# Output rows of odd batches tiled from row 64 on, and tail tiles stored by one DMA over 128 partitions

## The chip, the cores and the metric

The kernel runs on one core of a Trainium2 chip. The metric is device time in microseconds (us), the median of several executions of the same program. One further execution is recorded by the hardware profiler; the profile and the trace are of that one.

## The reference

Eight batches of 576 positions pass through eight heads of linear attention (head width 64), and the result (8 x 576 x 512) through a spectral mixer.

```python
# attention, phi(x) = elu(x) + 1
kv  = einsum('bhsd,bhse->bhde', phi(k), v);  z = sum(phi(k), axis=2)
x   = einsum('bhsd,bhde->bhse', phi(q), kv) / (einsum('bhsd,bhd->bhs', phi(q), z) + 1e-6)
# mixer, on x as [batch, 576, 512]
X   = rfft(x, axis=1)                 # the first 64 modes are kept
Y_m = X_m @ (w_r[m] + 1j * w_i[m])    # 64 modes, 512 x 512 each, complex
u   = x + irfft(Y)
out = u + relu(u @ w_ch)              # float32
```

The mode weights are the bulk of the input: 128 matrices of 512 x 512.

## The kernel before

**Row tiles.** A batch has 576 rows. Its first 512 are cut into four main tiles of 128: tile `jj` holds rows jj, jj+4, jj+8 and so on, so that one partition of `x_main[b]` holds four consecutive rows. The last 64 rows of two neighbouring batches share one tail tile: the even batch in partitions 0 to 63, the odd batch in partitions 64 to 127. `x_tail[i // 2]` holds two tail tiles side by side in a partition. There are 32 main and 4 tail tiles.

**First part (up to about 105 us).** Batch by batch, q, k and v are loaded by POOL's DMA queue, the features are formed, and q is turned (`qT`). `form_x` (L250) multiplies `qT` with the batch's kv, and its L262 takes the reciprocal of the denominators into `rd_all[b]`, row by row in the tiling above. `transform` makes the 64 Fourier modes of x from this.

**Modes (L335).** The weights stream in by POOL's queue (L115), 512 KB per half mode, into eight buffers, after twelve early ones. A load is issued when PE has used the buffer it goes to. For each mode PE multiplies the real and the imaginary weights (L348), DVE or ACT copies the result out (L362 or L364), and PE sorts it into `YT` (L366). The last four modes are in a fixed order, with filler matmuls (L333) between their halves. Mode 63 is done in another form (L386).

**Channel products (L466).** Between the modes, for each of the 36 tiles, PE multiplies `qT` with kv once more (L146), DVE divides by multiplying with `rd_all` (L479), ACT casts (L486), PE transposes (L489), DVE copies out (L491), PE multiplies with w_ch (L494) and ACT copies the product out (L502). The place of these instructions among those of the modes is chosen by a scheduler from its own costs and the waits; each engine then runs its own list strictly in order. Only what is marked as kept in program order stays where the source has it.

**Row products (L509).** Once modes 0 to 55 are in `YT`, each batch's rows are multiplied with w_ch (L517) and transposed (L521) into `YZ[b]`: 56 modes, real and imaginary, make 112 partitions. The last eight modes follow after mode 63 (L658, L668) and are distributed by eight small DMAs (L672).

**Output (L605).** For each of 18 pairs of tiles, PE adds E (L577) and the inverse transform of the second half of `YZ` (L536) in PSUM, ACT applies relu (L588), PE adds the inverse transform of the first half (L536), DVE adds x (L617 or L622), and `store` (L590) writes the pair. The inverse transform's matrix `inv_sb` is the stationary operand; its columns are sorted so that a tile takes 128 (or, for each half of a tail tile, 64) adjacent ones. The 16 pairs of main tiles leave by SP's queue, one DMA each, but the first and last pair in two; the two pairs of tail tiles leave in two DMAs each, of 64 partitions:

```python
for hf in range(2):
    (nc.sync, nc.gpsimd)[hf].dma_start(
        out=out[2 * i + hf : 2 * i + 4 : 2, 512:S, :].rearrange("b r d -> r b d"),
        in_=x_tail[i // 2][hf * 64 : hf * 64 + 64, :, :],
    )
```

The tail pairs come before the last main pair of batches 3 and 7.

Of the kernel before, what the change touches and what calls it, by code (L numbers as in the profile page):

```python
# [10 lines left out]
F32 = mybir.dt.float32  # L11
# [5 lines left out]
NJ = 9  # L17
NP = 64


def _dft_consts(S: int, NM: int, NL: int, NB: int):

    m = np.arange(NM)
    s_cols = np.concatenate([4 * np.arange(128) + jj for jj in range(4)] + [512 + np.arange(NP)])
    s_rows = np.concatenate([s_cols, s_cols[512:]]).reshape(5, 128).T
    ang = 2.0 * np.pi * s_rows[:, :, None] * m / S
    fwd = np.concatenate([np.cos(ang), -np.sin(ang)], axis=2)

    scale = np.where(m == 0, 1.0, 2.0) / S
    ang = 2.0 * np.pi * np.outer(m, s_cols) / S  # L30
    inv = np.empty((NM, 2, S), dtype=np.float64)
    inv[:, 0, :] = np.cos(ang) * scale[:, None]
    inv[:, 1, :] = -np.sin(ang) * scale[:, None]
    pick = np.zeros((128, 16), dtype=np.float16)
    for quad in range(4):
        for c in range(16):
            pick[quad * 32 + c, c] = 1.0

    inv0 = np.zeros((NL, 2, NB, S), dtype=np.float64)
    inv0[:, :, 0, :] = inv[NM - NL :]  # L40
    return (
        fwd.astype(np.float16), inv.reshape(2 * NM, S).astype(np.float16),
        inv0.reshape(2 * NL * NB, S).astype(np.float16), pick,
    )
# [3 lines left out]
def kernel(  # L48
# [10 lines left out]
    nc = tc.nc  # L59

    B, H, S, Dh = q.shape
# [4 lines left out]
    NJJ = 4  # L66
# [38 lines left out]
    kv_all = [xpool.tile([128, 2, 2, 65], F16, tag="kv", bufs=B, name=f"kv{b}") for b in range(B)]  # L105
    rd_all = [xpool.tile([128, 5, 2, 4], F32, tag="rd", bufs=B, name=f"rd{b}") for b in range(B)]
# [29 lines left out]
        pool, tag, bufs = (wpool, "w", W_KEEP) if kk < n_keep else (wpre, "wp", W_PRE)  # L136
        w_in.setdefault(kk, []).append(w_load(kk, half, pool, tag, bufs))

    def num_matmuls(num, orow, qT, kv_sb, jj, pinned=False):
        cols = slice(jj, 512, NJJ) if jj < NJJ else slice(512, NJ * NP)  # L140
        for hpp in range(2):
            for h2 in range(2):
                for hpo in range(2):
                    rows = slice(hpo * 64, hpo * 64 + 64)
                    c0 = (hpp * 2 + h2) * 65
                    mm = nc.tensor.matmul(  # L146
                        num[hpo][orow, c0 : c0 + 65], qT[rows, hpp, h2, cols], kv_sb[rows, hpp, h2, :]
                    )
                    if pinned:
                        pin(mm)  # L150
        return [n[orow, 0:260].rearrange("p (c n) -> p c n", c=4) for n in num]

    def q_view(t):
        return t.rearrange("p (c t s) -> p c t s", c=2, t=2)

    qT_all = [q_tile(f"qT{b}") for b in range(B)]
# [93 lines left out]
    def form_x(b, jj):  # L250
        if jj == 0:
            x16s[b] = (
                sA.tile([128, NJJ, D], F16, tag="x16", bufs=2, name=f"x16_{b}"),
                sA.tile([128, D], F16, tag="x16t", bufs=2, name=f"x16t_{b}"),
            )
        tail = jj == NJJ
        orow = HALVES[b % 2] if tail else slice(0, 128)
        num = psA.tile([128, 2, 512], F32, tag="big", bufs=3, name=f"num{b}_{jj}")
        num_matmuls([num[:, o] for o in range(2)], orow, q_view(qT_all[b]), kv_all[b], jj, True)
        nv = num[orow, :, 0:260].rearrange("p o (c n) -> p o c n", c=4)  # L260
        rden = rd_all[b][orow, jj]
        pin(nc.vector.reciprocal(out=rden, in_=nv[:, :, :, 64]))  # L262
        dst = x16s[b][1][orow, :] if tail else x16s[b][0][:, jj, :]
        pin(
            nc.vector.tensor_tensor(  # L265
                out=dst.rearrange("p (o c d) -> p o c d", o=2, c=4),
                in0=nv[:, :, :, 0:64],
                in1=rden.unsqueeze(3).broadcast_to([64 if tail else 128, 2, 4, Dh]),
                op=ALU.mult,
            )  # L270
        )
# [162 lines left out]
    for kk in range(n_early):  # L434
# [3 lines left out]
    sW = ctx.enter_context(tc.tile_pool(name="sW", bufs=1))  # L438
    x_main = [sW.tile([128, NJJ, D], F32, tag="x_main", bufs=B, name=f"x_main{b}") for b in range(B)]
    x_tail = [  # L440
        sW.tile([128, 2, D], F32, tag="x_tail", bufs=B // 4, name=f"x_tail{i}") for i in range(B // 4)
    ]
    YZ = [sW.tile([128, 2, D], F16, tag="YZ", bufs=B, name=f"YZ{b}") for b in range(B)]
    E0: dict[int, object] = {}

    def x_of(t: int):
        if t < B * NJJ:
            return x_main[t // NJJ][:, t % NJJ, :]
        i = t - B * NJJ
        return x_tail[i // 2][:, i % 2, :]  # L450
# [10 lines left out]
    def bank(name: str, shape=(128, D), dtype=F32):  # L461
        return psB.tile(list(shape), dtype, tag="bank", bufs=4, name=name)
# [3 lines left out]
    def channel_product(t: int):  # L466

        num = [bank(f"nw{t}_{o}") for o in range(2)]
        tail = t >= B * NJJ
        if tail:  # L470
            i = t - B * NJJ
            parts = [(2 * i + h, NJJ, slice(h * 64, h * 64 + 64)) for h in range(2)]
        else:
            parts = [(t // NJJ, t % NJJ, slice(0, 128))]
        x = x_of(t)
        for b, jj, orow in parts:
            nv = num_matmuls(num, orow, q_view(qT_all[b]), kv_all[b], jj)
            for o in range(2):
                nc.vector.tensor_tensor(  # L479
                    out=x[orow, o * 256 : o * 256 + 256].rearrange("p (c d) -> p c d", c=4),  # L480
                    in0=nv[o][:, :, 0:64],
                    in1=rd_all[b][orow, jj, o].unsqueeze(2).broadcast_to([64 if tail else 128, 4, Dh]),
                    op=ALU.mult,
                )
        x16 = sW.tile([128, D], F16, tag="x16w", bufs=2, name=f"x16w{t}")
        nc.scalar.copy(out=x16, in_=x)  # L486
        xT_ps = bank(f"xTp{t}", [128, NDC, 128], F16)
        for c in range(NDC):
            nc.tensor.transpose(xT_ps[:, c, :], x16[:, c * 128 : c * 128 + 128], id16)  # L489
        xT = sW.tile([128, NDC, 128], F16, tag="xTw", bufs=2, name=f"xTw{t}")  # L490
        nc.vector.tensor_copy(out=xT, in_=xT_ps)  # L491
        e_ps = bank(f"eps{t}")
        for c in range(NDC):
            nc.tensor.matmul(  # L494
                e_ps, xT[:, c, :], wch16[:, c, :], start=(c == 0), stop=(c == NDC - 1)
            )
        need = {t // NJJ} if not tail else {2 * i, 2 * i + 1}
        for b in sorted(need):
            if b not in E0:
                E0[b] = q_tile(f"E0_{b}")  # L500
        for cols, dst in e0_parts(t):
            nc.scalar.copy(out=dst, in_=e_ps[:, cols])  # L502
# [29 lines left out]
    def add_inverse(n: int, i: int, t: int, half: int, what: int = BOTH):  # L532

        acc = accs[n][:, i]
        mm = lambda o, l, r: on_bank(
            n, {i}, nc.tensor.matmul(o, l, r, start=False, stop=True, skip_group_check=True)  # L536
        )
        if t < B * NJJ:
            parts = [(t // NJJ, slice(0, 128), slice(t % NJJ * 128, t % NJJ * 128 + 128))]
        else:  # L540
            p = t - B * NJJ
            parts = [(2 * p + h, slice(h * 64, h * 64 + 64), slice(512, 576)) for h in range(2)]
        for b, r, sel in parts:
            if what == BOTH:
                mm(acc[r, :], inv_sb[:, sel], YZ[b][:, half, :])
                continue
            if what & EARLY:
                mm(acc[r, :], inv_sb[: 2 * NE, sel], YZ[b][: 2 * NE, half, :])
            if what & LATE:
                mm(acc[r, :], inv0_sb[:, sel], last[:, half, :])  # L550
# [39 lines left out]
    def store(t: int, n_t: int):  # L590
        if t < B * NJJ:
            b, jj = divmod(t, NJJ)
            nc.sync.dma_start(
                out=out[b, 0:512, :].rearrange("(r j) d -> r j d", j=NJJ)[:, jj : jj + n_t, :],
                in_=x_main[b][:, jj : jj + n_t, :],
            )
            return
        i = t - B * NJJ
        for hf in range(2):
            (nc.sync, nc.gpsimd)[hf].dma_start(  # L600
                out=out[2 * i + hf : 2 * i + 4 : 2, 512:S, :].rearrange("b r d -> r b d"),
                in_=x_tail[i // 2][hf * 64 : hf * 64 + 64, :, :],
            )

    def finish(n: int):  # L605
        acc = accs[n]
# [47 lines left out]
    for h in range(2):  # L654
        cols = slice(h * hw, h * hw + hw)
# [67 lines left out]
```

## Time and profile before

| | |
|---|---|
| median of 4 runs | 432.47 us (431.88 to 433.25) |
| the profiled execution | 433.15 us, of which the profile's span is 431.2 us |
| busy share of the span | PE 70%, PE weight loads 36%, DVE 41%, ACT 34%, POOL 22% |
| DMA moved | 92.38 MB, mean 214 GB/s |
| mean granted TensorE clock | 0.708 |
| stores of x_main | 14 of 512 KB and 4 of 256 KB on SP |
| stores of x_tail | 2 of 256 KB on SP, 2 of 256 KB on POOL |

PE is TensorE's matmul stream and PEld its weight loads; DVE is VectorE, ACT ScalarE, POOL GpSimd; SP only issues DMAs here. A line such as L494 is a line of the kernel above. In the forty slices of the span a digit is a share in tenths. The granted clock is the share of TensorE's full clock. A line of the timeline gives the start, the duration, the engine, the source line, what is written and read, and the count; the bracket at its end is the engine's idle time before it, with what ended it.

### The profile page before, as it was taken

Reading aid. Unit: us, or ns where it says so; the run is one execution under the profiler, and the core shown is the slowest. Engines: PE = TensorE matmul, PEld = TensorE weight load, DVE = VectorE, ACT = ScalarE, POOL = GpSimd, SP = SyncE. Lnnn points to the kernel's source line nnn. Section 1 sums busy time; section 2 is a strip of 40 time slices with the busy share of each in tenths; the row PEclk is TensorE's granted clock in tenths of the full one; section 3 lists DMA queues with packets and bytes.
Section 4 is the critical chain, followed back from the end, with each engine's and each line's share of the span. In section 5 each row is a group of like instructions: output and inputs, shape, how many; then the busy total and the mean of one; then the engine's idle time right before and its main releaser. Section 6 shows DMA issues by size and latency. Waiting matters only on the chain.

```text
span 431.2 us, 6233 instructions
## 1 busy us (share of the span) xinstructions
PE 301.4 (70%) x2551; PEld 154.1 (36%) x2551; DVE 176.6 (41%) x333; ACT 146.9 (34%) x227; POOL 92.8 (22%) x167
## 2 busy tenths in 40 slices
PE   0358676787028777676776778777787758998991
PEld 0346555673004233322322223223232217834340
DVE  1699998954004232322232223223223312201893
ACT  3687666621003222222223222222222311301781
POOL 4232322222112221211222112112112121210100
PEclk9999866665558766657568565555556666998997
DMA  8999999999999999999999999999999999993797
GB/s 147 207 208 209 209 209 209 212 213 216 221 211 213 215 213 213 214 213 213 213 215 214 213 212 215 213 214 214 213 213 213 215 214 213 214 212 73 295 328 278
DMA packets 35707, 92.38 MB, mean 214 GB/s; under 512 B 3168, under 2 KB 16480, under 8 KB 35680
## 3 DMA queue, kind: packets, MB, share of 16 engines
q0 software_dynamic: 32160, 82.52, 98.4%
q1 hardware_dynamic: 3520, 9.47, 6.0%
q8 instruction: 20, 0.33, 0.3%
q14 instruction: 7, 0.06, 0.0%
HBM read 164.07 MB, written 9.44 MB: 402 GB/s over the span
## 4 chain that ended last, share of the span: by engine, by line
DMA 68%; PE 16%; DVE 6%; issue 5%; ACT 2%; POOL 1%; DVEq 0%; POOLq 0%; ACTq 0%
DMA wi<-in_moe_w_i_dram 35%; DMA wr<-in_moe_w_r_dram 21%; PE P L348 4%; DMA pick_sb<-row_pick 4%; DMA q<-in_q_dram 4%; PE acc L536 3%; DMA k<-in_k_dram 3%; PE z L517 2%; DVE x L265 2%; PE acc L577 2%; PE eps L494 1%; PE yp L521 1%; PE yt L366 1%; DVE qe L195 1%; ACT ke L182 1%
## 5 line engine op out<-in xcount | busy, mean ns | idle before, releaser
L494 PE MATMUL eps<-wch,xTw 128*128 128x512 f16 x144 | 62.7, 585 | 3.4 <-DVE xTw L491 3.2
L502 ACT CAST E<-eps 128x512 f16<-128x512 f32 (+1 forms) x40 | 21.3, 544 | 121.0 <-PE eps L494 121.0
L348 PE MATMUL P<-wi,xt_c 128*32 128x512 bf16 x252 | 45.5, 565 | 22.2 <-DMA wi<-in_moe_w_i_dram 22.1
L115 POOL DMA_DIRECT2D wi<-in_moe_w_i_dram x65 | 34.5, 532 | 121.7 <-PE P L348 83.1
L348 PE MATMUL P<-wr,xt_c 128*32 128x512 bf16 x252 | 45.3, 577 | 21.8 <-DMA wr<-in_moe_w_r_dram 19.9
L115 POOL DMA_DIRECT2D wr<-in_moe_w_r_dram x64 | 34.0, 532 | 120.0 <-PE P L348 93.7
L479 DVE TENSOR_TENSOR x_main<-nw,rd 128x256 f32<-128x256 f32 x64 | 24.2, 420 | 73.1 <-PE nw L146 73.0
L362 DVE CAST ys<-P 128x512 f16<-128x512 f32 x32 | 22.0, 688 | 60.3 <-PE P L348 60.2
L348 PEld LDWEIGHTS <-xt_c 128*32 128x32 bf16 x504 | 24.0, 163 | 57.6 <-issue 28.8
L146 PEld LDWEIGHTS <-qT 64*128 64x128 f16 (+1 forms) x640 | 21.4, 126 | 55.7 <-issue 40.1
L364 ACT CAST ys<-P 128x512 f16<-128x512 f32 x31 | 18.2, 586 | 62.0 <-PE P L348 61.7
L366 PE MATMUL yt<-pick_sb,ys 128*128 128x16 f16 x252 | 16.8, 177 | 30.7 <-DMA pick_sb<-row_pick 20.4
L491 DVE COPY xTw<-xTp 128x512 f16<-128x512 f16 x36 | 15.2, 423 | 43.9 <-PE xTp L489 43.9
L366 PEld LDWEIGHTS <-ys 128*128 128x128 f16 x252 | 12.9, 105 | 51.1 <-issue 24.3
L146 PE MATMUL num<-kv,qT 64*128 64x65 f16 (+1 forms) x320 | 13.8, 227 | 23.2 <-ACT kv L242 20.1
L494 PEld LDWEIGHTS <-xTw 128*128 128x128 f16 x144 | 14.6, 123 | 38.1 <-issue 22.2
L182 ACT ACTIVATE qe<-q 128x1152 f16<-128x1152 f16 x16 | 17.7, 1156 | 22.4 <-DMA q<-in_q_dram 22.4
L211 PE MATMUL qTp<-id,qe 128*128 128x128 f16 x144 | 16.5, 309 | 12.1 <-DVE qe L195 11.7
L486 ACT CAST x16w<-x_main 128x512 f16<-128x512 f32 x32 | 19.8, 619 | 13.4 <-DVE x_main L479 13.4
L265 DVE TENSOR_TENSOR x<-num,rd 128x512 f16<-128x512 f32 x32 | 22.1, 692 | 1.1
L489 PE MATMUL xTp<-id,x16w 128*128 128x128 f16 x144 | 19.4, 278 | 4.0 <-ACT x16w L486 3.6
L588 ACT ACTIVATE acc<-acc 128x512 f32<-128x512 f32 x36 | 19.1, 581 | 5.5 <-PE acc L536 3.8
(69 smaller groups left out, 385.0 us busy)
## 6 DMA issues: line engine op xcount, KB each, us to landing
wr<-in_moe_w_r_dram POOLq DMA_DIRECT2D x64, 512.0 KB, 18.3
wi<-in_moe_w_i_dram POOLq DMA_DIRECT2D x63, 512.0 KB, 18.4
out_dram<-x_main SPq DMA_DIRECT2D x14, 512.0 KB, 5.0
q<-in_q_dram POOLq DMA_DIRECT2D x8, 576.0 KB, 13.1
k<-in_k_dram POOLq DMA_DIRECT2D x8, 576.0 KB, 14.5
v<-in_v_dram POOLq DMA_DIRECT2D x8, 576.0 KB, 16.7
out_dram<-x_main SPq DMA_DIRECT2D x4, 256.0 KB, 3.6
wch<-in_moe_w_ch_dram POOLq DMA_DIRECT2D x1, 512.0 KB, 20.4
```

What stands on the lines that cost most here:

```text
L115: tc.keep_in_program_order(nc.gpsimd.dma_start(out=w[:, dcs], in_=rows_of[:, dcs, :]))
L146: mm = nc.tensor.matmul(num[hpo][orow, c0 : c0 + 65], qT[rows, hpp, h2, cols], kv_sb[rows, hpp, h2, :])
L182: pin(nc.scalar.activation(out=ev[:, c], in_=heads(nm, b)[:, c], func=AF.Exp))
L265: nc.vector.tensor_tensor(out=dst.rearrange("p (o c d) -> p o c d", o=2, c=4), in0=nv[:, :, :, 0:64], in1=rden.unsqueeze(3).broadcast_to([ ...
L348: mm = nc.tensor.matmul(P[i][dc * 32 : dc * 32 + 32, :], xt_cols(dc, t, kk), w[:, dc, i * pw : i * pw + pw], start=(t == 1), stop=(t == 0) ...
L362: nc.vector.tensor_copy(out=dst, in_=P[i])
L366: mm = nc.tensor.matmul(yt_ps[:, ec, kk % 8, :], st[:, ec * 128 : ec * 128 + 128], pick_sb)
L479: nc.vector.tensor_tensor(out=x[orow, o * 256 : o * 256 + 256].rearrange("p (c d) -> p c d", c=4), in0=nv[o][:, :, 0:64], in1=rd_all[b][or ...
L486: nc.scalar.copy(out=x16, in_=x)
L489: nc.tensor.transpose(xT_ps[:, c, :], x16[:, c * 128 : c * 128 + 128], id16)
L494: nc.tensor.matmul(e_ps, xT[:, c, :], wch16[:, c, :], start=(c == 0), stop=(c == NDC - 1))
L502: nc.scalar.copy(out=dst, in_=e_ps[:, cols])
```

## The change

Odd batches' main tiles start at row 64 (`BASE`), and their remaining rows are 0 to 63. In the flat view of the output (`out_rows`, 4608 rows), the last 64 rows of an even batch and the first 64 of the next are adjacent, so a tail tile is 128 consecutive rows. Each tail pair is stored by one DMA on SP; POOL stores nothing.

The first part keeps its tiling for all batches, so the stored reciprocals no longer match the odd batches' tiles: their channel products take their own, one `[128, 4]` (or 64 rows) reciprocal per half, 40 in all. `inv_sb` is no longer sorted; a main tile takes every fourth column of it, from row 64 on for odd batches.

```diff
-    ang = 2.0 * np.pi * np.outer(m, s_cols) / S
+    ang = 2.0 * np.pi * np.outer(m, np.arange(S)) / S
...
-    def num_matmuls(num, orow, qT, kv_sb, jj, pinned=False):
-        cols = slice(jj, 512, NJJ) if jj < NJJ else slice(512, NJ * NP)
+    def rows_of(jj: int, base: int = 0):
+
+        if jj < NJJ:
+            return slice(base + jj, base + 512, NJJ)
+        return slice(512, S) if base == 0 else slice(0, base)
+
+    def num_matmuls(num, orow, qT, kv_sb, cols, pinned=False):
...
-        num_matmuls([num[:, o] for o in range(2)], orow, q_view(qT_all[b]), kv_all[b], jj, True)
+        num_matmuls(
+            [num[:, o] for o in range(2)], orow, q_view(qT_all[b]), kv_all[b], rows_of(jj), True
+        )
...
+    BASE = (0, 64)
+    out_rows = out.rearrange("b s d -> (b s) d")
...
-            nv = num_matmuls(num, orow, q_view(qT_all[b]), kv_all[b], jj)
+            nv = num_matmuls(num, orow, q_view(qT_all[b]), kv_all[b], rows_of(jj, BASE[b % 2]))
             for o in range(2):
+                rden = rd_all[b][orow, jj, o]
+                if b % 2 == 1:
+                    rden = sW.tile([128, 4], F32, tag="rdw", bufs=4, name=f"rdw{t}_{o}")[orow]
+                    nc.vector.reciprocal(out=rden, in_=nv[o][:, :, 64])
                 nc.vector.tensor_tensor(
...
-                    in1=rd_all[b][orow, jj, o].unsqueeze(2).broadcast_to([64 if tail else 128, 4, Dh]),
+                    in1=rden.unsqueeze(2).broadcast_to([64 if tail else 128, 4, Dh]),
...
-            parts = [(t // NJJ, slice(0, 128), slice(t % NJJ * 128, t % NJJ * 128 + 128))]
+            b, jj = divmod(t, NJJ)
+            parts = [(b, slice(0, 128), rows_of(jj, BASE[b % 2]))]
...
-            parts = [(2 * p + h, slice(h * 64, h * 64 + 64), slice(512, 576)) for h in range(2)]
+            parts = [
+                (2 * p + h, slice(h * 64, h * 64 + 64), rows_of(NJJ, BASE[h])) for h in range(2)
+            ]
...
+            r0 = b * S + BASE[b % 2]
             nc.sync.dma_start(
-                out=out[b, 0:512, :].rearrange("(r j) d -> r j d", j=NJJ)[:, jj : jj + n_t, :],
+                out=out_rows[r0 : r0 + 512, :].rearrange("(r j) d -> r j d", j=NJJ)[:, jj : jj + n_t, :],
...
-        for hf in range(2):
-            (nc.sync, nc.gpsimd)[hf].dma_start(
-                out=out[2 * i + hf : 2 * i + 4 : 2, 512:S, :].rearrange("b r d -> r b d"),
-                in_=x_tail[i // 2][hf * 64 : hf * 64 + 64, :, :],
-            )
+        nc.sync.dma_start(
+            out=out_rows.rearrange("(i r) d -> r i d", i=B // 2)[512:640, i : i + 2, :],
+            in_=x_tail[i // 2],
+        )
```

## The prediction

> **What bounds the kernel now.** I read first the page's forty slices, to see which resource is full when.
>
> ```profile
> PEclk9999866665558766657568565555556666998997
> DMA  8999999999999999999999999999999999993797
> GB/s 147 207 208 209 209 209 209 212 213 216 221 211 213 215 213 213 214 213 213 213 215 214 213 212 215 213 214 214 213 213 213 215 214 213 214 212 73 295 328 278
> ```
>
> The DMA engines are full for 36 of 40 slices: this is the weight stream, at one fixed rate of 213 GB/s (by the trace one 512 KB load lands every 2.45 us, without a gap, the last at 394.06). Slice 37 is the hand-over (73 GB/s), and the last three store the output. So the end is set by three things: the arrival of the last weights, what lies between them and the first store, and the stores. Next, the windows by stage (us, busy time and count of PE, PEld, DVE, ACT, POOL, then granted clock, DMA share, GB/s).
>
> ```profile
> 346.50:357.00 10.50, 5.72 (x36) 2.07 (x36) 1.81 (x3) 1.17 (x2) 2.11 (x4) 0.66 1.06 213
> 357.00:364.00 7.00, 6.80 (x25) 4.89 (x26) 1.11 (x3) 1.17 (x2) 0.53 (x1) 0.52 1.06 212
> 364.00:379.00 15.00, 14.27 (x95) 12.00 (x95) 3.68 (x8) 4.69 (x8) 4.23 (x8) 1.00 1.06 213
> 379.00:391.50 12.50, 12.20 (x75) 4.25 (x73) 2.01 (x3) 0.59 (x1) 0.00 (x0) 1.00 1.04 206
> 391.50:394.40 2.90, 2.11 (x35) 1.26 (x35) 0.00 (x0) 0.00 (x0) 0.00 (x0) 1.00 0.29 52
> 394.40:398.50 4.10, 3.61 (x17) 2.14 (x18) 0.65 (x2) 1.63 (x4) 0.56 (x2) 0.59 0.00 0
> 411.00:422.00 11.00, 11.00 (x56) 4.71 (x55) 9.91 (x10) 8.98 (x18) 0.63 (x1) 1.00 0.94 338
> ```
>
> PE idles 4.8 us of 10.5 just before 357, but from 357 to 391.5 it is packed (the row products L517/L521, then modes 57 to 62 with their fillers L333). It only just keeps up with the weights, as the timeline says in the bracketed waits of the last mode:
>
> ```profile
> 391.61 0.65 PE L386 MATMUL y_last<-xt_c,wr 128*128 128x16 bf16 x16 [0.27 <-DMA wr<-in_moe_w_r_dram]
> 393.45 0.94 PE L386 MATMUL y_last<-xt_c,wi 128*128 128x16 bf16 x16 [0.55 <-DMA wi<-in_moe_w_i_dram]
> 394.71 1.89 PE L658 MATMUL zl<-wch,YT 128*128 128x256 f16 x8 [0.32 <-DVE YT L397]
> ```
>
> 0.27 + 0.55 us, and 0.24 on the weight load of the last quarter: PE may be about 1.1 us late before the end moves. Then the stores, in windows of 1 us (same columns), and their issues:
>
> ```profile
> 411.50:412.50 1.00, 1.00 (x7) 0.41 (x6) 0.93 (x2) 0.78 (x3) 0.51 (x1) 1.00 0.28 100
> 412.50:413.50 1.00, 1.00 (x6) 0.49 (x5) 1.00 (x1) 0.78 (x2) 0.00 (x0) 1.00 0.98 203
> 418.00:419.00 1.00, 1.00 (x8) 0.52 (x6) 0.93 (x2) 0.78 (x3) 0.00 (x0) 1.00 1.04 422
> 425.00:426.00 1.00, 0.00 (x0) 0.00 (x0) 0.00 (x0) 0.00 (x0) 0.00 (x0) 0.55 1.01 242
> 428.00:429.00 1.00, 0.00 (x0) 0.00 (x0) 0.00 (x0) 0.00 (x0) 0.00 (x0) 0.50 0.74 279
> ```
> ```profile
> 411.11 0.68 SPq L600 DMA_DIRECT2D out_dram<-x_tail  x1
> 423.23 0.63 SPq L600 DMA_DIRECT2D out_dram<-x_tail  x1
> 423.95 3.32 SPq L593 DMA_DIRECT2D out_dram<-x_main  x2
> ```
>
> The engines are as full at 203 GB/s (412.5, the first x_tail half alone) as at 422 (whole x_main pairs). DVE is done at 424.4, but packets run to 429.5: the backlog that the x_tail stores left is the end of the kernel. PE makes a pair in 1.29 us and the DMA stores a pair in 1.28 to 1.30, so a backlog once made is never worked off.
>
> [...] the trace shows the halves overlapping in part and neither running fast. [...] the trace's clock spells are multiples of 3.41 us.
>
> **The change, part by part.**
>
> (1) Stores. By the trace's packet records the 128 packets of 2 KB of the first SP half took 1.28 us of sixteen engines (151 ns at the median) and POOL's half 1.10, together 2.38; the second pair 1.11 + 0.87 = 1.98. The same 2 KB packets of the last x_main tiles, over 128 partitions, take 84 ns. The new store is 256 of them: 256 x 0.085 / 16 = 1.36 us. Engine time saved: 1.02 + 0.62 = 1.64. POOL's half began 2.4 us after its issue, the SP half 1.34 after; the joint store has SP's delay only. Issue: 0.65 us for 128 descriptors in two per partition; for 256, between 0.65 and 1.3. Queue: issued at 411.11, first packet 412.45 to 413.05, done 413.8 to 414.4; eight x_main pairs at 1.295 follow to 424.2 to 424.8; the second tail, issued at 423.23, starts at 424.6 to 425.2, ends 425.9 to 426.6; behind it on SP are the two single x_main stores (issued about 424.5 and 424.9 instead of 423.95 and 425.57), 0.69 each: 427.3 to 428.0, against 429.55. Gain 1.55 to 2.25; I take 1.9.
>
> (2) Reciprocals. 32 on 128 rows and 8 on 64, as 40 of the kind
>
> ```profile
> L262 DVE RECIPROCAL rd<-num x40: 186/197/211, 24.5 to 99.1; 128x8 f32<-128x8 f32 x32, 64x8 f32<-64x8 f32 x8
> ```
>
> 8 us of DVE from 137 to 357, where DVE is 29% busy (61.7 of 214 us) and the weight stream sets the pace: nothing directly. Uncovered, it would be 8 us.
>
> (3) What they move. A product of an odd batch takes about 0.4 us longer from L146 to L486, and the built program's order answers: on PE the last two channel products stand one to two modes later. Before, the last L494 group comes inside mode 54; after, one comes in mode 55 and the last behind mode 56's second half. All counts on PE are the same. Followed through with the trace's durations: mode 56's first half starts at 357.20 as now (weights landed at 357.16), 0.6; then L366 and L489, 0.7, to 358.5; its second half waits for weights to 359.6, 0.6; L494 at half clock 1.8, to 362.1; then the first four z/yp pairs, the first mostly at half clock (2.5), the others 1.8: 370. Now they take 5.2 + 3.6 us on both sides of that half, and mode 57 starts at 367.25. So PE is 2.7 late there, is packed from there to mode 62, and has 1.1 of slack: the last mode ends 1.6 later. Queued behind it are L397, L658, every L536 and all stores, which move alike. The weights are not delayed: loads go out up to 3 us later, but took 13.6 to 16.1 us to land after issue at that point, so their queue never empties.
>
> Part of this comes back. Because PE waits at 391.5 to 394.4, it has clock 0.59 from 394.4 to 398.5, and L658 runs at 213 ns instead of 107: 8 x 0.107 = 0.85 us; the first four L536 take 1.30 instead of 0.86, of which I count 0.3. A PE that arrives late has no such gap. Net loss: 1.6 - 1.15 = 0.45. Bounds: 0 to -0.8, if the clock rises a window earlier and the lag is absorbed; +1.7, if it rises one 3.4 us window later (1.3 more); +2.8, if also nothing comes back.
>
> (4) Weights of L536 read with a stride of 4. They take 99 ns now, beside matmuls of 215 ns. L146 reads qT with just that stride, and in the groups by form takes as long as the dense ones:
>
> ```profile
> L146 PEld LDWEIGHTS <-qT 64*128 64x128 f16 x240 | 7.4, 124 | 20.8 <-issue 20.7
> L494 PEld LDWEIGHTS <-xTw 128*128 128x128 f16 x140 | 14.3, 124 | 37.6 <-issue 21.9 <-DVE xTw L491 13.6
> ```
>
> Hidden behind the matmul until a load exceeds 215 ns; beyond that, 64 loads times the excess. I take 0.
>
> Sum: -1.9 + 0.45 = -1.45. The profiled execution took 433.15 (span 431.2, 1.95 around it), so 431.7 for its like. It is 0.7 above the median of the four runs; on the median 432.47 the same step gives 431.0.
>
> **The rivals.**
>
> A, the sum: 431.0; chance 0.60, own range 430.2 to 431.6.
>
> B, a bigger gain: PE's lag is wholly absorbed or the clock repays it (0 to -0.8) while the stores gain 2 or more: 432.47 - 2.3 = 430.2 and down to 429.7; chance 0.13. [...] Against: L658 repays only if PE arrived late.
>
> C, a wash: the clock rises a window later, +1.7 against -1.9, or mode 57 is later than I count: 432.3; chance 0.17. For it: PE is packed at 97% and slack is 1.1. Against: 360.3 to 363.7 should be busy enough after the change too.
>
> D, slower: TensorE becomes the bound before the last mode. The two late products and the half clock hold mode 57 back by 4 us or more, the last mode ends 2.8 us late and nothing comes back: 432.47 + 2.8 - 1.9 = 433.4. It decides where the last mode's delay exceeds the store gain by 0.9, so from 397.1 on in the trace's time, against 394.3 now. Chance 0.06.
>
> E, the store doesn't do what it says: two runs of 2 KB per partition still take 150 ns each, or the issue of 256 descriptors starves the engines by 1 us twice. Then 2.4 us of engine time for 256 packets stays and 0.45 is lost: 432.9; chance 0.04. Against it: the single x_main stores, same packets, at 84 ns.
>
> **How the numbers follow.** Predicted is A, 431.0. Within 0.2% (0.86 us) a measurement of this kernel can hardly tell a change: the limits are 431.6 and 433.3. Faster takes A, save its margin, and B: 0.70. Same takes most of C, half of E and A's margin: 0.21. Slower takes D and what is left: 0.09. The range 429.7 to 432.7 leaves out D, the far part of E and the best of B.
>
> **What would show it.** Right: x_tail packets at about 85 ns and 390 GB/s or more in the window where they run, DVE's end to last packet under 4 us instead of 5.1, no DMA issue of POOL after its YZ transfers; L494 inside mode 56 and mode 57's first L348 at about 370; no DMA wait left at L386; clock 1.00 in the 4 us after the last mode; L536's weight loads still about 100 to 130 ns. Wrong: a half-clock window behind 363.7, or stores that leave gaps behind the issue of an x_tail store.

## The result, and the profile after

| | before | after |
|---|---|---|
| median of the runs | 432.73 us (431.65 to 435.12, 53 runs) | 431.42 us (430.35 to 432.85, 33 runs) |
| ratio, 95% interval | 1 | 0.9969 (0.9961 to 0.9977) |
| the profiled execution, and its span | 433.15, 431.2 us | 431.23, 429.1 us |

The kernel is 0.31% faster, 1.3 us, with an interval of 1.0 to 1.7 us. Every kernel further down was measured beside executions of the kernel before, and its ratio is to those; it is not the quotient of two medians and differs from it by up to 0.12% here, so differences of that size are read with care. The forty slices of the profile after, in the same three rows as before:

```profile
PEclk9999866565558775555866578555656685999998
DMA  8999999999999999999999999999999999995697
GB/s 147 207 208 209 209 209 210 210 214 215 222 212 214 213 213 213 214 213 213 213 213 214 213 213 214 214 214 213 213 213 213 212 214 213 214 213 110 237 373 296
```

The weight stream is as it was, 36 full slices, most of them at about 213 GB/s. What differs is at the end: slice 37 of the clock reads 9 where it read 8, slice 40 reads 8 instead of 7, and slice 39 stores at 373 GB/s rather than 328. The windows by stage (us, busy time and count of PE, PEld, DVE, ACT, POOL, granted clock, DMA share, GB/s):

```profile
346.50:357.00 10.50, 7.46 (x52) 2.55 (x50) 3.10 (x11) 1.79 (x3) 1.58 (x3) 0.69 1.06 213
357.00:364.00 7.00, 5.95 (x27) 3.42 (x28) 2.10 (x4) 1.91 (x4) 1.58 (x3) 0.50 1.06 213
364.00:379.00 15.00, 15.00 (x95) 13.47 (x94) 4.09 (x9) 5.05 (x9) 2.11 (x4) 1.00 1.06 213
379.00:391.50 12.50, 11.71 (x77) 4.48 (x74) 0.69 (x1) 1.17 (x2) 1.59 (x3) 1.00 1.02 203
391.50:394.40 2.90, 2.86 (x33) 1.38 (x30) 1.32 (x2) 0.00 (x0) 0.00 (x0) 1.00 0.35 64
394.40:398.50 4.10, 3.40 (x37) 2.31 (x35) 0.65 (x2) 1.97 (x5) 0.91 (x2) 1.00 0.00 0
```

The last channel products stand later: PE has 7.46 us of work from 346.5 to 357 where it had 5.72, and 5.95 where it had 6.80 from there to 364. From 364 to 379 it has no gap (it was busy for 14.27 of 15), but then idles 0.8 us up to 391.5 (it was 0.3): a wait behind mode 59 has moved from the one window into the other, as the section on the prediction shows. From 391.5 to 394.4 PE is busy for 2.86 of 2.9 us, where it was 2.11. In the next window the clock is full and 37 matmuls are begun, not 17. PE's timeline, with the last channel product, the first half of mode 57, the two halves of mode 63 and the last modes' row product:

```profile
360.15 1.89 PE L507 MATMUL eps<-wch,xTw 128*128 128x512 f16 x4
...
369.50 0.48 PE L355 MATMUL P<-wr,xt_c 128*32 128x512 bf16 x4
...
393.34 0.64 PE L393 MATMUL y_last<-xt_c,wr 128*128 128x16 bf16 x16
...
394.46 0.64 PE L393 MATMUL y_last<-xt_c,wi 128*128 128x16 bf16 x16
395.41 1.05 PE L674 MATMUL zl<-wch,YT 128*128 128x256 f16 x8 [0.32 <-DVE YT L404]
```

The waits for weights at mode 63 are gone. PE starts the last row product (L674, before L658) 0.70 us later than before, and does it in 1.05 instead of 1.89 us. Then the stores, in windows of 1 us (same columns), and SP's timeline:

```profile
411.20:412.20 1.00, 1.00 (x6) 0.52 (x5) 0.93 (x2) 0.78 (x3) 0.00 (x0) 1.00 0.70 266
412.20:413.20 1.00, 1.00 (x7) 0.47 (x6) 1.00 (x1) 0.78 (x2) 0.00 (x0) 1.00 1.07 406
418.20:419.20 1.00, 1.00 (x10) 0.48 (x8) 0.93 (x2) 0.79 (x2) 0.00 (x0) 1.00 0.86 344
426.90:427.90 1.00, 0.00 (x0) 0.00 (x0) 0.00 (x0) 0.00 (x0) 0.00 (x0) 0.50 0.04 14
```
```profile
410.72 0.39 SPq L616 DMA_DIRECT2D out_dram<-x_tail  x1
422.85 0.38 SPq L616 DMA_DIRECT2D out_dram<-x_tail  x1
423.45 1.19 SPq L610 DMA_DIRECT2D out_dram<-x_main  x2
```

The window of the tail store moves 406 GB/s, where the half alone moved 203. Between 418.2 and 419.2 the engines are no longer full (0.86, before 1.04 in the like window), so the backlog is gone. From 426.9 on only the last packets of one engine are left (0.04), where before the engines were still 0.74 busy between 428 and 429. Five points of the two profiled executions show where the 2.1 us of the span went (us from the start):

| | before | after | difference |
|---|---|---|---|
| L658, after L674: the last modes' row product begins | 394.71 | 395.41 | +0.70 |
| first inverse transform that uses the last modes (L536, after L549) | 397.21 | 397.07 | -0.14 |
| issue of the first output store | 400.20 | 399.79 | -0.41 |
| issue of the second tail store | 423.23 | 422.85 | -0.38 |
| last packet | 429.55 | 427.48 | -2.07 |

From the second tail store's issue to the last packet it was 6.32 us and is 4.63: 1.69 of the 2.07 lie there. A single pair of executions says this; the experiments say what holds on the median.

### The profile page after: what moved, and what is told of

Same layout as the page of the kernel before. It is cut to its first block, busy times and chain, and to the rows that moved or that the text cites. A ratio compares the mean times of both kernels' runs of the same rounds, so it can differ in the third digit from the quotient of the medians.

```text
span 429.1 us, 6238 instructions
## 1 busy us (share of the span) xinstructions
PE 294.4 (69%) x2551; PEld 154.2 (36%) x2551; DVE 182.0 (42%) x373; ACT 146.7 (34%) x227; POOL 91.5 (21%) x165
## 4 chain that ended last, share of the span: by engine, by line
DMA 67%; PE 17%; issue 7%; DVE 4%; ACT 2%; POOL 1%; DVEq 0%; POOLq 0%; ACTq 0%
DMA wi<-in_moe_w_i_dram 33%; DMA wr<-in_moe_w_r_dram 22%; DMA k<-in_k_dram 11%; PE acc L549 4%; PE P L355 3%; PE z L530 2%; PE zl L340 2%; PE acc L593 2%; PE eps L507 2%; PE yp L534 1%; DVE x L272 1%; ACT ke L187 1%; DVE k L194 0%; ACT qT L223 0%; POOL q L169 0%
## 5 line engine op out<-in xcount | busy, mean ns | idle before, releaser
L355 PE MATMUL P<-wi,xt_c 128*32 128x512 bf16 x252 | 41.5, 554 | 27.6 <-DMA wi<-in_moe_w_i_dram 27.5
L355 PE MATMUL P<-wr,xt_c 128*32 128x512 bf16 x252 | 41.7, 572 | 23.6 <-DMA wr<-in_moe_w_r_dram 21.5
L492 DVE TENSOR_TENSOR x_main<-nw,rd 128x256 f32<-128x256 f32 x32 | 12.1, 419 | 33.7 <-PE nw L151 33.7
L491 DVE RECIPROCAL rdw<-nw 128x4 f32<-128x4 f32 (+1 forms) x40 | 5.5, 171 | 39.3 <-PE nw L151 39.2
```

The source lines that it names most:

```text
L355: mm = nc.tensor.matmul(P[i][dc * 32 : dc * 32 + 32, :], xt_cols(dc, t, kk), w[:, dc, i * pw : i * pw + pw], start=(t == 1), stop=(t == 0) ...
```

## The stores, taken apart

The theory: packets out of 64 neighbouring partitions are slow. In the trace of before those of the SP half took 151 ns at the median, and packets of the same 2 KB in the last x_main stores, over 128 partitions, 84. The rival: two DMAs, two issues and two queues cost the time, whatever partitions they take. Three kernels keep everything else of the kernel after and store the tail pair differently. The first goes back to the old halves:

```diff
-        nc.sync.dma_start(out=out_rows.rearrange(...)[512:640, i : i + 2, :], in_=x_tail[i // 2])
+        rows = out_rows.rearrange("(i r) d -> r i d", i=B // 2)
+        for hf in range(2):
+            (nc.sync, nc.gpsimd)[hf].dma_start(
+                out=rows[512 + hf * 64 : 576 + hf * 64, i : i + 2, :],
+                in_=x_tail[i // 2][hf * 64 : hf * 64 + 64],
+            )
```

> The changed kernel, with its tail pair stored again as two DMAs of partitions 0 to 63 (SP) and 64 to 127 (POOL); tiling, reciprocals and order of the products stay as changed. Theory (the gain is the store over all partitions, 1.7 us by the two traces): the gain is lost, 433.1, no faster than the kernel before; the SP half's packets take about 150 ns again and the last packet ends 3.5 us or more after the last issue's data are ready. Rival (the gain is a side effect of the new order on PE and the clock it keeps): 431.4, as the changed kernel.

It took 433.12 us (22 runs), ratio to before 1.0006 (0.9994 to 1.0019). So the joint store is the whole gain: 1.0006 less 0.9969 is 0.37% or 1.6 us, and all else that the change did comes to +0.3 us on the median, within -0.3 to +0.8, which can't be told from nothing.

The second stores the even partitions with SP and the odd ones with POOL, still 64 partitions per DMA:

```diff
-                out=rows[512 + hf * 64 : 576 + hf * 64, i : i + 2, :],
-                in_=x_tail[i // 2][hf * 64 : hf * 64 + 64],
+                out=rows[512 + hf : 640 : 2, i : i + 2, :],
+                in_=x_tail[i // 2][hf::2],
```

> The changed kernel, with its tail pair stored as two DMAs of 64 partitions each, even ones on SP and odd ones on POOL: as many DMAs, descriptors and queues as before the change, but each half reaches over the whole partition range. Theory (what is slow is a store out of the lower or the upper 64 partitions alone): packets of 2 KB at 85 to 90 ns, 431.4 to 431.9, the upper end if POOL's later start leaves a gap. Rival (what was slow is the second queue, POOL's late start and two issues): 433.1, as with the halves.

432.09 us (22 runs), ratio 0.9982 (0.9973 to 0.9990). The windows of 1 us that hold the first store, first of the kernel with halves, then of the one with even and odd partitions:

```profile
412.00:413.00 1.00, 1.00 (x6) 0.52 (x5) 0.93 (x2) 0.78 (x3) 0.00 (x0) 1.00 1.02 209
```
```profile
412.00:413.00 1.00, 1.00 (x7) 0.48 (x5) 0.93 (x2) 0.94 (x2) 0.00 (x0) 1.00 1.03 397
```

With as many partitions, bytes and issues, and full engines in both, nearly twice the bytes move, 397 GB/s against 209. By the packet records a 2 KB packet of SP's DMA takes 152 ns from the lower half and 86 ns from even partitions; the two DMAs together occupy the engines for 1.27 + 1.10 = 2.37 us in the one, 0.70 + 0.68 = 1.38 in the other, and 1.38 to 1.40 in the joint store, in every profile of a kernel that has it. So it matters which 64 partitions a DMA takes; what makes packets from neighbouring ones slow is not shown. The two kernels also write different rows of the output with one DMA, every second one or neighbours; but the joint store writes 128 neighbouring rows with packets of 86 ns, so neighbouring rows alone don't make packets slow.

That gives 0.24% (1.0006 to 0.9982, 1.0 us) of the 0.37%. From the second tail store's issue on SP to the last packet it was 6.63 us with halves, 5.12 with even and odd partitions, and 4.63 with one DMA (4.56 to 4.94 in the eight profiles taken of kernels that have it). The remaining half us or less goes with the two issues. SP's timeline, again first with halves, then with even and odd partitions:

```profile
422.36 0.64 SPq L618 DMA_DIRECT2D out_dram<-x_tail  x1
423.08 3.80 SPq L610 DMA_DIRECT2D out_dram<-x_main  x2
```
```profile
422.18 0.64 SPq L618 DMA_DIRECT2D out_dram<-x_tail  x1
422.91 1.36 SPq L610 DMA_DIRECT2D out_dram<-x_main  x2
```

An issue for 64 partitions takes 0.64 us, the joint one 0.38. The first packet of the even partitions came 1.29 us after the issue began, that of the joint store 0.90, and POOL's packets began 0.7 us after SP's. The stretch for the last two x_main issues is SP waiting between and in them; it is 3.80 us where packets in front are slow, and 1.36 with even partitions. To separate POOL's late start from the second issue itself, the third kernel issued both on SP:

```diff
-            (nc.sync, nc.gpsimd)[hf].dma_start(
+            nc.sync.dma_start(
```

> The changed kernel, its tail pair stored as two DMAs of 64 partitions, even and odd ones, both on SP. Theory ([...] what the same split over SP and POOL lost is POOL's late start): ratio 0.997, as with one DMA, the time from the issue of the second tail store to the last packet 4.6 to 4.8 us. Rival (two issues cost in any case): ratio 0.998, 5.1 us, as on SP and POOL.

432.28 us (22 runs), ratio 0.9985 (0.9970 to 0.9999), where the theory expected about 0.997. Packets were at 85 ns, so it was not the partitions: two issues in a row took SP 1.41 us instead of 0.39, and from the start of the second pair's issues to the last packet it was 5.31 us, where that theory had 4.6 to 4.8 and its rival 5.1. The kernel after took 431.51 us beside it. So the second issue costs about as much on SP as on POOL, though the intervals are too wide to rank the two.

Theory and rival both hold, in shares that are about 1.0 us for the partitions and 0.5 for the second DMA; the second share is the less certain, since the intervals of 0.9982 and 0.9969 touch. One DMA is the best of the four (0.9969 against 0.9982, 0.9985 and 1.0006), but most of the loss came from which partitions each half took, not from there being two.

## The front part, taken apart

The rest of the change makes PE late. The theory from the prediction: the reciprocals shift the order on PE, the last mode ends later, and the clock gives most of it back. The rival: the lag costs what it is long. The first kernel leaves out the 40 new reciprocals, so odd batches are divided by the stored values of other rows; by its program, the order on PE is that of before.

```diff
-                if b % 2 == 1:
+                if False and b % 2 == 1:
```

> The changed kernel without its 40 new reciprocals: odd batches are divided by the stored reciprocals, which belong to other rows. This gives PE the order of the kernel before, so that the last channel product is done inside mode 54. Theory of the prediction (PE's lag costs 0.45 us net): 431.0, mode 57 starts at about 367.3 and the last mode waits for weights again. Rival (the lag is repaid by the clock that PE then keeps after the last mode, as in the profiled execution of the changed kernel): 431.4 to 431.8, with half clock after the last mode.

431.37 us (9 runs), ratio 0.9955 (0.9938 to 0.9971), from 430.1 to 433.1. The two waits of mode 63 are back as before, 0.27 and 0.55 us, and so is the half clock behind them. From 394.4 to 398.5 its window reads

```profile
394.40:398.50 4.10, 3.60 (x19) 2.11 (x20) 0.65 (x2) 1.39 (x3) 0.33 (x1) 0.51 0.00 0
```

In this execution the half clock lasted 6.8 us, to 401.3; the execution took 433.12 us, the longest of its nine. Without the reciprocals the kernel can be faster and can be slower; its median is that of after, and its ratio is 0.14% lower, with intervals that overlap. Nine executions don't decide between the two theories.

A kernel that gives the right reciprocals without new instructions was tried next: the first part, too, tiles odd batches from row 64 on, with nine instead of five tables for the Fourier modes. The computation is complete, and PE has the order of before.

```diff
-    s_rows = np.concatenate([s_cols, s_cols[512:]]).reshape(5, 128).T
+    odd = np.concatenate([NP + 4 * np.arange(128) + jj for jj in range(4)])
+    s_rows = np.concatenate([s_cols, np.arange(NP), odd]).reshape(9, 128).T
...
-        num_matmuls(..., rows_of(jj), True)
+        num_matmuls(..., rows_of(jj, NP * (b % 2)), True)
...
-                    o, x16[:, jj, dc::NDC], fwd_sb[:, jj, :], start=(jj == 0), stop=False
+                    o, x16[:, jj, dc::NDC], fwd_sb[:, jj + 5 * (b % 2), :], start=(jj == 0), stop=False
...
-                if b % 2 == 1:
-                    rden = sW.tile([128, 4], F32, ...)
-                    nc.vector.reciprocal(out=rden, in_=nv[o][:, :, 64])
```

> The changed kernel with the first part of odd batches tiled from row 64 on as well: its stored reciprocals then fit the odd batches' tiles, the 40 new reciprocals go, and the Fourier matrix gets four more tables (128 KB more to load at the start). All of the reference is computed. PE has the order of the kernel before. Theory (the lag of PE that the reciprocals bring costs 0.3 to 0.6 us of the store's gain): ratio to the kernel before 0.9955 to 0.996, 430.9 to 431.1 where the kernel before takes 432.7. Rival (the lag is repaid by the clock): ratio 0.997, as the changed kernel.

431.85 us (22 runs), ratio 0.9970 (0.9955 to 0.9985), where the theory of a lag that costs time expected 0.9955 to 0.9960. It spreads from 429.85 to 433.53. The profiled execution is the fastest of all: mode 63 began at 391.15, 2.2 us before that of after, the clock happened to stay full, and the last packet was at 426.30. But the median is no better than that of after. Taking the lag away brings PE's waits back at mode 63. Whether the clock then falls in the slower of its executions is open: those have no trace.

If the waits are the trouble, fillers in them should help. The next kernel adds to the last one an extra filler behind mode 62 and two between the halves of mode 63:

```diff
-            keep_warm(3)
+            keep_warm(4 if kk == NM - 2 else 3)
...
-        keep_warm(3)
+        keep_warm(5)
```

> The kernel with the odd batches shifted from the first part on (no new reciprocals, PE in the order of the kernel before), with three more fillers in PE's waits for the last weights: two between the halves of mode 63, one ahead of it. Theory (without the fillers that kernel spread from 429.9 to 433.5 because the clock fell in some executions): all executions now lie near the fast end, 430.0 to 430.6, ratio 0.994 to 0.995. Rival (the spread has another cause): 431.8 and as wide, ratio 0.997.

431.00 us (13 runs), ratio 0.9956 (0.9937 to 0.9975), from 430.3 to 432.8: not the narrow band that was expected. In its profiled execution the clock was full to the end; the time went elsewhere. The last weight packets came at 394.75 us (393.73 before, 393.64 after), and PE waited for them at 395.22. So a late end of the weight stream can be part of the spread; one execution doesn't say how large a part.

Last, the kernel after keeps its order, but the lag is shortened by taking two fillers out behind the first half of each of the modes 60 to 62:

```diff
-                keep_warm(6)
+                keep_warm(4)
```

> The changed kernel with four instead of six fillers behind the first half of modes 60 to 62: 6 x 0.2135 = 1.28 us less of PE between mode 59 and the last mode, where it is 0.7 to 1.1 us late. Theory (PE is the bound there): the last mode ends at about 394.3, held by the weights, and the end comes 0.7 us earlier, ratio 0.9953, if the clock stays full; ratio 0.998 if PE's new wait lets the clock fall behind it. Rival (PE's lag costs nothing on the median): 0.997, no change against the changed kernel.

430.90 us (16 runs), ratio 0.9957 (0.9941 to 0.9973). The kernel after on the same chip took 431.51 (below). Both were measured once more, side by side (the text below says "each half"; the kernel is the one of the diff above, with the first half alone):

> The kernel after with four rather than six fillers in each half of modes 60 to 62, once more, beside the kernel after on the same chip. If the lag of PE ahead of the last mode still costs the kernel after some tenths of a us, which the earlier medians 430.9 and 431.5 suggest, it is again 0.4 to 0.7 us below the kernel after: ratio to the kernel before 0.995 to 0.996. If those medians differed by chance, the two are within 0.2 us of each other here.

431.29 us (22 runs), ratio 0.9960 (0.9948 to 0.9972), against 431.55 of the kernel after: 0.26 us less, which is nearer the 0.2 of chance than the 0.4 to 0.7 of the theory. The two sessions make 0.61 and 0.26; resampling the runs of each gives 0.2 to 1.0 us for their mean. With the shifted kernel with fillers (431.00, 0.9956) it is the fastest complete kernel here, by a little, with ratio intervals that overlap those of after. What fewer fillers do is plain in its traces: in the second session mode 63 began at 391.69, with one wait of 0.29 us for weights left, and the clock stayed full.

```profile
394.40:398.50 4.10, 3.60 (x23) 2.22 (x24) 0.81 (x3) 2.87 (x6) 1.80 (x4) 1.00 0.11 30
```

The kernel after itself, twice more as the companion of these runs:

> The changed kernel itself once more, beside the three others: 0.997. In its profile the last channel product lies inside mode 56 and mode 63 has no wait for weights; the clock behind the last mode may be full or half, which tells whether what the first profile showed there is the rule.

> The kernel after unchanged, for the comparison with the one with fewer fillers: 431.2 to 431.6 us, ratio to the kernel before 0.996 to 0.9975 under both theories.

431.51 us (20 runs), ratio 0.9959 (0.9945 to 0.9972), and 431.55 us (22 runs), ratio 0.9972 (0.9955 to 0.9988). The median is steady to 0.13 us over three sessions. In all three profiled executions of after the clock is full from mode 63 on.

## Does a wait at mode 63 cost clock, and the clock time?

Theory: PE's waits before 394.4 let the clock fall, and that costs time. Rival: these executions only look so. Both tests start from the kernel before. The first fills the waits, with the filler lines of the last diff but one.

> The kernel before with three more filler matmuls where PE waits for the last weights: two between the halves of mode 63 and one ahead of it, 0.64 us in waits of 0.82 us. Nothing of the change is in it. If PE's idle time there is what drops the clock, then the last mode ends where it did, the clock stays full behind it, and L658 and the first L536 are 0.8 to 1.15 us shorter: 431.6 to 431.9. If the clock drops all the same, or did so in the profiled execution only: 432.7, no difference.

432.30 us (14 runs), ratio 0.9997 (0.9985 to 1.0009). In the profiled execution the clock is full from 363.5 to 425.0 and the first inverse transform on the last modes begins at 396.41 rather than 397.21. It lies between the two expected times and decides for neither: the ratio shows no gain, its interval allows up to 0.6 us, and the plain median is 0.64 us below that of the executions of before beside it (432.94). Before loses the clock in the execution that was profiled; how often it does, and so what curing it is worth, stays open.

The second takes the three fillers between the halves of mode 63 out:

```diff
-        keep_warm(3)
```

> The kernel before without the three fillers between the halves of mode 63, so that PE waits 1.2 instead of 0.55 us there. Nothing of the change is in it. Theory (what PE idles before the last weights lowers the clock behind the last mode, for 3.4 us or for 6.8 us as in one profile): the last mode ends where it did, the half clock comes in every execution, and the time goes up by 0.3 to 1 us. Rival (the clock there is a matter of chance and costs nothing on the median): ratio 1.000.

434.09 us (14 runs), ratio 1.0024 (1.0007 to 1.0040). Its windows around mode 63 and PE's timeline:

```profile
391.50:394.40 2.90, 1.42 (x32) 1.08 (x32) 0.13 (x1) 0.00 (x0) 0.00 (x0) 0.78 0.25 46
394.40:398.50 4.10, 3.76 (x16) 2.13 (x17) 0.52 (x2) 1.79 (x4) 0.72 (x2) 0.50 0.00 0
```
```profile
393.29 0.95 PE L386 MATMUL y_last<-xt_c,wi 128*128 128x16 bf16 x16 [1.20 <-DMA wi<-in_moe_w_i_dram]
394.55 1.89 PE L657 MATMUL zl<-wch,YT 128*128 128x256 f16 x8 [0.32 <-DVE YT L396]
```

PE was busy for 1.42 of 2.9 us, the clock was half for 6.8 us from 393.1 on, L657 took 1.89 us, and the first store was issued at 401.18 instead of 400.20, although the last mode ended 0.16 us earlier. So a wait there does cost clock and time. The half clock came in a spell of 6.8 us here and of 3.4 us in the profile of before (394.39 to 397.80). PE was not idle ahead of it: in the 3.41 us from 389.71 to 393.12 it was busy for 2.07.

The other traces can be asked the same. In each of the fourteen profiles the clock changes only at points that lie whole multiples of 3.41 us apart. Between two such points around mode 63 and the first stores (384 to 404), PE was busy for 2.07 us here, 2.46 in before and 2.47 in the kernel without reciprocals, each time just ahead of the fall. In the eleven profiles whose clock stayed full there, the least is 2.54, in the shifted kernel with and without fillers. So the busy time between two points sets these profiles apart, if narrowly. It does not decide every fall: earlier in the kernel after a stretch with 1.83 us, from 244.7 on, was not followed by a fall, and one with 2.75 us was, in the kernel with even and odd partitions from 96.1 on.

## Why the prediction was right, step by step

**The base.** The forecast was 432.47 - 1.45 = 431.0. The change measured 1.3 us; the base was 0.26 too low, because four runs of before have a median of 432.47 and 53 runs one of 432.73. With that base the same sum gives 431.3, against 431.42.

**(1) Stores, predicted -1.9 (-1.55 to -2.25).** -1.6 on the medians of the kernel with halves and after, -1.69 in the profiles. The engine time was right: 1.36 us predicted for 256 packets, 1.38 to 1.40 measured. In the queue two terms were off, and they cancel. The issue was put at 0.65 to 1.3 us and the first packet 1.34 to 1.94 after it; the issue took 0.39 us and the first packet came after 0.90. With the backlog gone, the second tail store ran from 423.75 to 425.31, where 424.6 to 425.2 and 425.9 to 426.6 were worked out. But the last x_main store was put at 0.69 us and took 1.60, from 425.88 to 427.48: by the packet records fifteen of the sixteen engines are done by about 426.7 and one goes on alone, packet by packet of 84 ns. The window says the same (DMA share 0.06, one sixteenth):

```profile
426.70:427.40 0.70, 0.00 (x0) 0.00 (x0) 0.00 (x0) 0.00 (x0) 0.00 (x0) 0.50 0.06 23
```

Before, the engines ran out one after the other from 428.5 to 429.55. Why one engine is late was not tried.

**(2) Reciprocals, predicted nothing directly.** They are as they were priced: 40 of them, 168 ns in the mean for 128 rows, where 197 was taken. The instructions of that one line (least, median and most ns; the times between which they lie; the two shapes):

```profile
L491 DVE RECIPROCAL rdw<-nw x40: 151/182/186, 160.3 to 356.4; 128x4 f32<-128x4 f32 x32, 64x4 f32<-64x4 f32 x8
```

All lie before 357 under the weight stream. The only effect of theirs that these runs show is the order on PE; without them the ratio was 0.9955 and with them, in three sessions, 0.9959 to 0.9972.

**(3) What they move, predicted +1.6 and 1.15 of it back, net +0.45.** The order was right: the last channel product stands inside mode 56 and ends at 362.0 (362.1 was worked out). Mode 57 began at 369.50 where 370 was forecast and 367.25 was before: a lag of 2.25, not 2.7. Of it 1.55 was absorbed by the end, not 1.1, and the last mode ended 0.70 later, not 1.6. The term that was mis-sized, beside the lag itself, is the slack. It does not come from PE's idle 0.73 us behind mode 59, since that wait is in both kernels. The end of that wait and the start of mode 62, before and then after:

```profile
377.51 0.26 PE L366 MATMUL yt<-pick_sb,ys 128*128 128x16 f16 x4 [0.73 <-ACT ys L364]
387.24 0.47 PE L348 MATMUL P<-wr,xt_c 128*32 128x512 bf16 x4
```
```profile
379.76 0.26 PE L373 MATMUL yt<-pick_sb,ys 128*128 128x16 f16 x4 [0.74 <-ACT ys L371]
389.51 0.47 PE L355 MATMUL P<-wr,xt_c 128*32 128x512 bf16 x4
```

The lag is 2.25 and 2.27 us at these two points, so nothing has been made up. At the second half of mode 62 it is 2.14, at the first half of mode 63 1.73, at its second half 1.01 and at its end 0.7: all of it is made up where the kernel before waits for the last weights. The prediction looked in the right place but took the bracketed waits, 0.27, 0.55 and 0.24, where the starts show 0.41, 0.72 and 0.31, and 0.13 at mode 62. The brackets are shorter because the records of matmuls that follow without a wait overlap: after, mode 63 begins at 393.34, while the fillers ahead of it end at 393.50.

What comes back was right for L658 (0.84 against 0.85) and the first four L536 (0.27 against 0.3). So the profile's net is 0.70 - 0.84 - 0.27 = -0.41, as the issue of the first output store says too, and not +0.45; on the median it is +0.3 (-0.3 to +0.8). Both can hold if the clock gives its part back only against those executions of before that lose it behind mode 63, as the profiled one does. The prediction counted this part as sure; how often it is there is not shown. That the total came within 0.15 us of the forecast once the base is right is partly luck: the stores gained 0.3 less and the front part cost about 0.15 less than was predicted.

**(4) Weights of L536 with a stride, predicted 0.** In the groups by form, before and after:

```profile
L536 PEld LDWEIGHTS <-inv_sb 128*128 128x128 f16 x64 | 6.0, 99 | 8.7 <-issue 2.5
L549 PEld LDWEIGHTS <-inv_sb 128*128 128x128 f16 x64 | 6.9, 114 | 7.9 <-issue 2.1
```

114 ns instead of 99: with the stride a load takes 15 ns longer, which the prediction, with 124 ns for both kinds, did not have. It is still well under a matmul of 215 ns, and nothing of it shows: from 398.4 (before 398.8) on the matmuls of the first tiles begin 0.22 us apart in both profiles.

**The rivals.** A holds. B's lag that the clock repays came true in the profile (-0.41) but not on the median, and the stores gained 1.6 to 1.7 us, not 2. C and D needed a window of half clock behind 363.7: in the three profiles of after it is full from 364.1 or before. In the first of them PE was busy in all of the 3.41 us ahead of that rise, as it was ahead of the rise at 363.67 in before. E is refuted by packets of 86 ns and the issue of 0.39 us.

## What to carry to other kernels

Count a store's engine time from packet durations of the same partitions, not from bytes: 64 neighbouring partitions cost nearly as much engine time as 128 here, 1.27 us against 1.39. When work is moved on an engine that waits later, follow the lag to that wait by the start times of the instructions, since the bracketed waits add up to less than the slack, and see what the wait did to the clock: a late engine can run faster for not having waited (the last row product took PE 1.05 us instead of 1.89 here). A wait that both kernels have, as the one behind mode 59 (0.73 and 0.74 us), absorbs nothing. A gain on the profiled execution that rests on one clock window must be tested on the median.

## What was not expected

- One DMA from 128 partitions with two runs of 2 KB each (256 packets) is issued in 0.38 to 0.39 us; one of SP's from 64 partitions, with half as many packets, takes 0.63 to 0.70 us, whether the partitions are neighbours or not. x_main's 128 partitions with one run each take mostly 0.33 us.
- The end of the weight stream moves from execution to execution: the last weight packets ended between 393.45 and 394.10 us in three profiled executions of the kernel after, and between 393.27 and 394.75 over all kernels here, which is more than the 1.3 us that the change is worth. How much of the wider range is due to the kernels' different orders on PE stays open.
- Whether the clock falls behind mode 63 can't be read from the waits alone: it fell in before and without reciprocals, and stayed full in the profile of the shifted kernel, whose waits are as long (0.28 and 0.55 us). How often an execution of each kernel loses the clock stays open, since only few of them have a trace.
- At the end of the kernel after, one of the sixteen DMA engines works 0.8 us longer than the others, as told under the stores.
